# Attention and a gated two-layer block in one kernel: TensorE in written order, another order of loads, transposes and constants

## The chip, the cores and the metric

The kernel runs on one core of one Trainium2 chip. A core has five engines that run their own instruction streams and wait for each other by semaphores: TensorE (PE in the profile, its weight loads PEld), VectorE (DVE), ScalarE (ACT), GpSimd (POOL) and SyncE (SP), which here only issues DMAs. TensorE writes to PSUM, of which there are eight banks. The metric is the time of one execution on the device, in microseconds (us).

## What is computed

The input is q, k and v of 4 batches, 8 heads, 768 positions and 64 dimensions. Each head attends causally; heads 0, 2 and 6 ("retrieval") see all earlier positions, the other five ("streaming") only the first 4 positions and a window of 64. The result, 3072 rows of 512, goes through two dense layers with a swish between them.

```python
def _attn_ref(q, k, v, is_retrieval, n_sink, window):
    scores = scale * np.matmul(q, k.transpose(0, 1, 3, 2))
    ...
    stream_keep = causal & (is_sink | in_win)
    mask = np.where(retr[0, :, 0, 0, None, None], full_mask, stream_mask)
    scores = np.where(mask[None, :, :, :], scores, -1000000000.0)
    ...
    a = a / (np.sum(a, axis=-1, keepdims=True) + 1e-09)
    return np.matmul(a, v).astype(np.float32)

def _moe_ref(x, w_in, w_out, beta):
    h = x @ w_in                                   # 3072 x 512 by 512 x 2048
    g = h * (1.0 / (1.0 + np.exp(-beta * h)))
    return (g @ w_out).astype(np.float32)          # 2048 x 512
```

## The kernel before

The work is cut into eight units, one for each batch and half of the sequence (384 positions): unit 0 is batch 0, first half; unit 1 its second half, and so on. Even units have less attention than odd ones, since a first half sees fewer keys. For a unit there are these pieces:

- Loads. `load_qk` brings q and k of a pair of heads as two DMAs of 192 KB and casts each to bf16 (tiles `q2`, `k2`). `load_v` brings v by head and casts it on GpSimd into `vr` (retrieval) and `vs` (streaming, where the four first positions, `sk`, are copied into every block).
- `transpose_pair` turns q and k of a pair on TensorE by the identity `ident`, six matmuls into one PSUM tile, and copies it on VectorE to `QK`. For streaming heads VectorE then gathers the key blocks into `KX` in two copies, the second for the sinks. There are four pairs a unit.
- `scores_round` makes scores into a PSUM tile `sp`, ScalarE takes the exponential into `es`, VectorE multiplies it by a mask. `BURSTS` groups these rounds: three groups in an even unit, five in an odd one.
- `sums` adds up the exponentials on TensorE (the matrix `esel` puts each head's sum in a row of `misc`), VectorE takes the reciprocal `rec`, and five DMAs bring it to all partitions: three small ones from `rec` to `rd` in DRAM, then two of 384 KB from `rd` to `R`. SyncE issues them.
- `pv` multiplies the exponentials by v into two `sp` tiles; VectorE multiplies by `R` into `xT`, the unit's activations, in two instructions.
- `mm1` has 16 steps. A step is four matmuls into an `h` tile, ScalarE's tanh into `t`, and one instruction of VectorE, (t+1)*h, into `gT`. (The swish is written as a tanh, with beta halved, and the output is halved at the end.) An `h` buffer is free once `gT` has been made.
- `mm2` has 48 matmuls into an `o` tile, 16 for each of three blocks of 128 rows; then ScalarE copies `o` to `osb`, and SyncE issues the DMA of 256 KB to the output.

PSUM is split into two `sp` tiles of two banks, one `misc`, two `h` and one `o`. Both weight matrices are loaded once, in four slices of 1 MB each through the tile `wf`, and cast: `w_in` on VectorE, `w_out` on GpSimd.

After unit 0's attention, a loop runs nine times over 16 steps. In turn n, each step issues one step of unit n's `mm1`, three matmuls of unit n-1's `mm2`, and the pieces that `pieces_a(n + 1)` (transposes at steps 0 to 2, rounds from step 1, sums at 9, `pv` at 13 and 14) and `pieces_l(n + 2)` (loads) put at that step. This is the order in which the program is written. What each engine gets is decided by the scheduler of the layer below, which reorders the instructions by its own estimates of cost, on all engines, TensorE included, and puts in every wait. SyncE's queue also carries all loads but the first unit's k and four of its v loads, which ScalarE issues. Each DMA takes one of eight semaphores in turn, and waits until the DMA that had that semaphore before it has landed, whichever engine issued that one.

The program begins with unit 0's loads; the constants (`ident`, the masks, `esel`, `beta_h`) come after them.

Of the kernel before, what the change touches and what calls it, by code (L numbers as in the profile page):

```python
# [20 lines left out]
NQ = 384  # L21
# [31 lines left out]
def kernel(  # L53
# [29 lines left out]
    inp = pool("inp", 2)  # L83
# [25 lines left out]
    def load_qk(b, u, pi):  # L109
        ha, hb = PAIRS[pi]  # L110
        res = []
        for nm, src in (("q2", q), ("k2", k)):
            f = stg.tile([128, 2, TU, D], F32, name=nm + "f", bufs=4)
            eng = nc.scalar if (b, u, nm) == (0, 0, "k2") else nc.sync
            eng.dma_start(
                out=f,
                in_=bass.AP(src.tensor, src.offset + ((b * H + ha) * S + u * NQ) * D,
                            [[TU * D, 128], [(hb - ha) * S * D, 2], [1, TU * D]]),
            )
            c = inp.tile([128, TU, 2, D], BF16, name=nm)  # L120
            cast(nc.gpsimd if b > 0 and nm == "q2" else nc.vector, c.rearrange("p t a d -> p a t d"), f)
            res.append(c)
        qk_in[b, u, pi] = res
# [30 lines left out]

    for pi in range(NP):
        load_qk(0, 0, pi)
    for f in load_v(0, 0):
        f()
# [42 lines left out]

    beta_h = consts.tile([128, FO], F32, name="beta_h")
    nc.scalar.dma_start(out=beta_h, in_=moe_beta.rearrange("(fo fi) -> fi fo", fi=128))
    nc.vector.tensor_scalar(out=beta_h, in0=beta_h, scalar1=0.5, scalar2=None, op0=MULT)

# [5 lines left out]
    def load_w_in(s):  # L211
        f = stg.tile([128, 4, FS], F32, name="wf")
# [7 lines left out]
        cast(nc.vector, w_in_sb[:, :, s * FS:(s + 1) * FS], f)  # L220

    def load_w_out(s):
        f = stg.tile([128, 4, FS], F32, name="wf")
        nc.sync.dma_start(out=f, in_=moe_w_out[s * 512:(s + 1) * 512, :].rearrange("(fo fi) d -> fi fo d", fi=128))
        cast(nc.gpsimd, w_out_sb[:, s * 4:(s + 1) * 4, :], f)
# [4 lines left out]
    def transpose_pair(x, pi):  # L230
        b, u = x.b, x.u
        c2 = qk_in.pop((b, u, pi))
        if (b, u) == (0, 0):
            ps = ps_h.tile([128, 2, TU, 128], BF16, name="h")
        else:
            ps = ps_m.tile([128, 2, TU, 128], BF16, name="misc")
        for i, c in enumerate(c2):
            for t in range(TU):
                nc.tensor.transpose(ps[:, i, t, :], c[:, t, :, :].rearrange("p a d -> p (a d)"), ident)  # L239
        nc.vector.tensor_copy(  # L240
            out=QK[pi][:, :, u * NQ:(u + 1) * NQ].rearrange("d a (p t) -> d a p t", t=TU),
            in_=ps.rearrange("d a t p -> d a p t"))
# [84 lines left out]
    def sums(x):  # L327
# [23 lines left out]
        for j in range(TU):  # L351
            nc.sync.dma_start(out=rd[:, j, :], in_=rec[32 * j:32 * j + 8, :])
        R = rp.tile([128, NP, NQ], F32, name="R")
        src = rd[:]
        for i in range(2):
            nc.sync.dma_start(
# [29 lines left out]
    def mm1(x, fi):  # L386
        if fi == 0:
            x.gT = gp.tile([128, FO, NQ], BF16, name="gT")
        h = ps_h.tile([128, 512], F32, name="h")
# [7 lines left out]
    def mm2(x, step, last):  # L397
        for m in range(step * 3, step * 3 + 3):
            ns, fi = divmod(m, FO)
            if fi == 0:  # L400
                x.o = ps_s.tile([128, 2, 512], F32, name="sp")[:, 0, :] if last else ps_o.tile([128, 512], F32, name="o")
            nc.tensor.matmul(x.o, x.gT[:, fi, ns * 128:(ns + 1) * 128], w_out_sb[:, fi, :],  # L402
                             start=(fi == 0), stop=(fi == FO - 1))
            if fi == FO - 1:
                osb = op_.tile([128, d_model], F32, name="osb")
                nc.scalar.activation(out=osb, in_=x.o, func=AF.Copy, scale=0.5)  # L406
                r0 = x.b * S + x.u * NQ + ns * 128
                nc.sync.dma_start(out=out[r0:r0 + 128, :], in_=osb)
# [5 lines left out]
    def pieces_a(n):  # L414
# [3 lines left out]
        x = units[n]  # L418

        def t(pi):  # L420
            return lambda: transpose_pair(x, pi)

        def burst(bu):
            def f():
                for (pi, ri) in bu:
                    scores_round(x, pi, ri)
            return f
        bs = BURSTS[x.u]
        p = [(0, t(0)), (0, t(1)), (1, t(2)), (1, burst(bs[0])), (2, t(3))]
        rest = bs[1:]  # L430
        for i, bu in enumerate(rest):
            p.append((3 + (6 * i) // len(rest), burst(bu)))
        p.append((9, lambda: sums(x)))
        p += [(13, lambda: pv(x, 0)), (14, lambda: pv(x, 2))]
        return p

    def pieces_l(n):

        if n >= N:
            return []  # L440
        x = units[n]
        p = [(2 * pi, lambda pi=pi: load_qk(x.b, x.u, pi)) for pi in range(NP)]
        p += [(5 + i, f) for i, f in enumerate(load_v(x.b, x.u))]
        return p

    for s, f in pieces_a(0):
        f()
    for s in range(4):
        load_w_in(s)
    for s, f in pieces_l(1):  # L450
        f()
    for s in range(4):
        load_w_out(s)
    for n in range(N + 1):
        lists = [pieces_a(n + 1), pieces_l(n + 2)]
        for s in range(FO):
            for l in lists:
                for st, f in l:
                    if st == s:
                        f()  # L460
            if n < N:
                mm1(units[n], s)
            if n > 0:
                mm2(units[n - 1], s, n == N)
# [35 lines left out]
```

The softmax here doesn't subtract the row's maximum and nothing guards it: scores larger than these inputs give would overflow.

## Time and profile before

| | |
|---|---|
| median of 2 runs | 297.25 us (295.93 to 298.58) |
| the profiled execution | 295.16 us, of which 293.4 us are the span from its first to its last instruction |
| busy: PE, DVE, ACT, POOL | 244.4, 176.2, 131.5, 74.1 us |
| moved by DMA | 44.97 MB, 153 GB/s over the span |
| first transpose on TensorE | 10.50 us |
| first `rec` | 29.27 us |
| first `mm1` matmul | 42.28 us |
| `xT` of units 1, 2, 3 | 83.23, 107.54, 134.35 us |
| `mm2` of the last unit alone | 279.63 to 289.36 us |

Matmuls are pipelined, so the length that a row gives to one of them (331 ns for `mm1`) is not what it takes from the next; four `mm1` matmuls that follow each other take 0.65 us from start to start, three of `mm2` take 0.65. Rows give an engine's idle time before them and what ended it; such idle time costs something only where the engine is what the others wait for.

### The profile page before, as it was taken

The numbers are of one execution on the slowest core, as the hardware profiler recorded it, in microseconds if no ns is written. First come the engines' busy times: TensorE is split into PE (matmuls) and PEld (weight loads), VectorE is DVE, ScalarE is ACT, GpSimd is POOL, SyncE is SP. The second block draws the span as 40 slices with busy tenths as digits, with TensorE's granted clock in tenths as the row PEclk, the third lists the DMA queues.
The fourth block names the chain that finished last, engine by engine and source line by source line (L and its number), as shares of the span: only waits on it lengthen the run. The fifth ranks groups of instructions, "written<-read, shape, count | busy, mean of one in ns | idle before, by whom it ended". The sixth has DMA issues, their size and how long they took to land.

```text
span 293.4 us, 5696 instructions
## 1 busy us (share of the span) xinstructions
PE 244.4 (83%) x2196; PEld 128.0 (44%) x2196; DVE 176.2 (60%) x335; ACT 131.5 (45%) x217; POOL 74.1 (25%) x158
## 2 busy tenths in 40 slices
PE   0137129799799989998999979999999999999994
PEld 0124104454345534554455534554455455545541
DVE  1186429985848896627963696449754975353400
ACT  0123006743147529624644487336643684245421
POOL 1291001756342254103460261053000000000000
PEclk9999857999999999999999999999999999999999
DMA  7993699989796799087786879434014110500111
GB/s 217 179 236 101 157 243 275 266 298 330 170 234 183 173 270 264 4 185 198 179 222 153 197 187 224 95 87 143 36 42 106 38 38 8 140 36 36 38 71 71
DMA packets 75850, 44.97 MB, mean 153 GB/s; under 512 B 47984, under 2 KB 68656, under 8 KB 75824
## 3 DMA queue, kind: packets, MB, share of 16 engines
q1 hardware_dynamic: 69536, 43.04, 58.6%
q10 hardware_dynamic: 6288, 1.58, 3.0%
q8 instruction: 17, 0.28, 0.4%
q14 instruction: 9, 0.07, 0.1%
HBM read 38.22 MB, written 6.39 MB: 152 GB/s over the span
## 4 chain that ended last, share of the span: by engine, by line
PE 55%; DVE 18%; DMA 12%; ACT 5%; issue 3%; POOL 3%; SPq 1%; ACTq 0%; DVEq 0%; POOLq 0%
PE h L391 23%; PE o L402 17%; PE sp L382 5%; DMA k2f<-in_k_dram 4%; PE sp L402 4%; DVE gT L395 4%; PE misc L343 3%; DMA wf<-in_moe_w_in_dram 3%; PE sp L309 3%; ACT t L394 3%; DMA R<-rd 2%; DVE QK_214 L240 2%; DMA vf<-in_v_dram 2%; DVE xT L383 2%; POOL vs L103 1%
## 5 line engine op out<-in xcount | busy, mean ns | idle before, releaser
L391 PE MATMUL h<-xT,w_in_sb 128*128 128x384 bf16 x512 | 107.1, 331 | 17.3 <-DVE xT L383 13.4
L394 ACT ACTIVATE t<-h,beta_h 128x384 f32<-128x384 f32 x128 | 74.6, 586 | 104.1 <-PE h L391 102.3
L395 DVE SCALAR_TENSOR_TENSOR gT<-t,h 128x384 bf16<-128x384 f32 x128 | 69.9, 550 | 61.0 <-ACT t L394 60.4
L402 PE MATMUL o<-w_out_sb,gT 128*128 128x512 bf16 x336 | 92.3, 379 | 3.5 <-ACT osb L406 3.4
L391 PEld LDWEIGHTS <-w_in_sb 128*128 128x128 bf16 x512 | 46.1, 98 | 58.2 <-issue 25.4
L402 PEld LDWEIGHTS <-gT 128*128 128x128 bf16 x384 | 36.5, 98 | 37.4 <-issue 6.4
L103 POOL CAST vs<-vf 128x384 bf16<-128x384 f32 (+1 forms) x40 | 22.6, 574 | 47.1 <-DMA vf<-in_v_dram 33.1
L103 POOL CAST vr<-vf 128x192 bf16<-128x192 f32 x24 | 9.1, 386 | 52.2 <-DMA vf<-in_v_dram 51.7
L383 DVE TENSOR_TENSOR xT<-sp,R 128x768 bf16<-128x768 f32 x16 | 14.6, 950 | 10.8 <-DMA R<-rd 9.6
L406 ACT ACTIVATE osb<-o 128x512 f32<-128x512 f32 x21 | 12.5, 594 | 15.2 <-PE o L402 12.7
L103 POOL CAST vs<-sk 4x640 bf16<-4x640 f32 (+3 forms) x24 | 17.3, 745 | 0.0
L343 PEld LDWEIGHTS <-esel 128*32 128x32 bf16 x372 | 9.0, 97 | 7.4 <-issue 7.0
L402 PE MATMUL sp<-w_out_sb,gT 128*128 128x512 bf16 x48 | 10.8, 379 | 0.0
L382 PEld LDWEIGHTS <-vr 128*64 128x64 bf16 x108 | 7.8, 112 | 6.5 <-issue 5.0
L349 DVE RECIPROCAL rec<-misc 96x128 f32<-96x128 f32 x8 | 7.6, 954 | 4.8 <-PE misc L343 4.8
L382 PEld LDWEIGHTS <-vs 128*64 128x64 bf16 x260 | 8.6, 116 | 3.0 <-issue 3.0
L239 PE MATMUL h<-ident,q_104 128*128 128x128 bf16 x3 | 0.5, 298 | 10.5 <-DVE ident L164 10.5
L103 POOL CAST w_out_sb<-wf 128x2048 bf16<-128x2048 f32 x4 | 7.6, 1892 | 5.4 <-DMA wf<-in_moe_w_out_dram 5.4
L309 PE MATMUL sp<-QK_218 64*128 64x384 bf16 (+2 forms) x36 | 8.4, 302 | 0.3 <-ACT es_1_668 L311 0.3
L309 PE MATMUL sp<-QK_212 64*128 64x384 bf16 (+2 forms) x72 | 8.4, 304 | 0.3 <-ACT es_1_556 L311 0.3
L103 DVE CAST w_in_sb<-wf 128x2048 bf16<-128x2048 f32 x4 | 4.8, 1210 | 4.9 <-DMA wf<-in_moe_w_in_dram 4.1
L240 DVE COPY QK_212<-misc 128x768 bf16<-128x768 bf16 x7 | 6.6, 946 | 0.4 <-PE misc L239 0.4
(484 smaller groups left out, 266.7 us busy)
## 6 DMA issues: line engine op xcount, KB each, us to landing
q2f<-in_q_dram SPq DMA_DIRECT2D x32, 192.0 KB
R<-rd SPq DMA_DIRECT2D x16, 384.0 KB
out_dram<-osb SPq DMA_DIRECT2D x24, 256.0 KB
k2f<-in_k_dram SPq DMA_DIRECT2D x28, 192.0 KB
vf<-in_v_dram SPq DMA_DIRECT2D x20, 224.0 KB
wf<-in_moe_w_out_dram SPq DMA_DIRECT2D x4, 1024.0 KB
vf<-in_v_dram SPq DMA_DIRECT2D x16, 192.0 KB
vf<-in_v_dram SPq DMA_DIRECT2D x24, 96.0 KB
```

Of the source, the lines that this page charges most:

```text
L103: eng.tensor_copy(out=dst, in_=src)
L240: nc.vector.tensor_copy(out=QK[pi][:, :, u * NQ:(u + 1) * NQ].rearrange("d a (p t) -> d a p t", t=TU), in_=ps.rearrange("d a t p -> d a p t"))
L309: nc.tensor.matmul(o[j][0], o[j][1], o[j][2], start=True, stop=True)
L343: nc.tensor.matmul(sm[32 * j:32 * j + 32, 0:128], esel[:, hpos, :, :].rearrange("p a b -> p (a b)"), e, start=(done[j] == 0), stop=(done[j ...
L349: nc.vector.reciprocal(rec, sm[0:96, 0:128])
L382: nc.tensor.matmul(a, l, r, start=st, stop=sp)
L383: nc.vector.tensor_mul(x.xT[:, p0:p0 + 2, :], o[:, :, 0:NQ], x.R[:, p0:p0 + 2, :])
L391: nc.tensor.matmul(h[:, 0:NQ], w_in_sb[:, pi, fi * 128:(fi + 1) * 128], x.xT[:, pi, :], start=(pi == 0), stop=(pi == NP - 1))
L394: nc.scalar.activation(out=t, in_=h[:, 0:NQ], func=AF.Tanh, scale=beta_h[:, fi:fi + 1])
L395: nc.vector.scalar_tensor_tensor(out=x.gT[:, fi, :], in0=t, scalar=1.0, in1=h[:, 0:NQ], op0=ADD, op1=MULT)
L402: nc.tensor.matmul(x.o, x.gT[:, fi, ns * 128:(ns + 1) * 128], w_out_sb[:, fi, :], start=(fi == 0), stop=(fi == FO - 1))
L406: nc.scalar.activation(out=osb, in_=x.o, func=AF.Copy, scale=0.5)
```

## The change

TensorE's instructions are issued in the order of the program (`manual_schedule` with that engine); the other engines are scheduled as before. The loop is written anew. A `slot` runs 16 steps of one unit's `mm1`, of another's `mm2`, or of both; the first two slots have `mm1` alone, then there is one with unit 0's `mm2` alone, and from unit 2 on both go together. Transposes stand a slot ahead of the scores that use them, `rec` at step 10, both halves of `pv` at step 14. Where a slot has `mm1` alone, every third `h` is taken from the `o` bank; where it has `mm2` alone, `o` is taken from the `h` banks. Constants stand ahead of all loads; q and k of unit 1 ahead of `w_in`. `rd` and `R` are issued by ScalarE. Some casts change engines.

```diff
-    inp = pool("inp", 2)
+    inp = pool("inp", 4)
...
-            cast(nc.gpsimd if b > 0 and nm == "q2" else nc.vector, c.rearrange("p t a d -> p a t d"), f)
+            cast(nc.gpsimd if (b, u) == (0, 1) or b > 0 and nm == "q2" else nc.vector, c.rearrange("p t a d -> p a t d"), f)
...
-    for pi in range(NP):
-        load_qk(0, 0, pi)
-    for f in load_v(0, 0):
-        f()
...
+    for pi in range(NP):
+        load_qk(0, 0, pi)
     beta_h = consts.tile([128, FO], F32, name="beta_h")
...
+    for f in load_v(0, 0):
+        f()
...
-        f = stg.tile([128, 4, FS], F32, name="wf")
+        f = stg.tile([128, 4, FS], F32, name="wf", bufs=3)
...
-        cast(nc.vector, w_in_sb[:, :, s * FS:(s + 1) * FS], f)
+        cast(nc.vector if s % 2 else nc.gpsimd, w_in_sb[:, :, s * FS:(s + 1) * FS], f)
...
-        if (b, u) == (0, 0):
+        if b == 0:
             ps = ps_h.tile([128, 2, TU, 128], BF16, name="h")
...
-        nc.vector.tensor_copy(
+        cast(
+            nc.scalar if (b, u) == (0, 0) and pi % 2 else nc.vector,
...
-            nc.sync.dma_start(out=rd[:, j, :], in_=rec[32 * j:32 * j + 8, :])
-        R = rp.tile([128, NP, NQ], F32, name="R")
+            nc.scalar.dma_start(out=rd[:, j, :], in_=rec[32 * j:32 * j + 8, :])
+        R = rp.tile([128, NP, NQ], F32, name="R", bufs=1)
...
-            nc.sync.dma_start(
+            nc.scalar.dma_start(
                 out=R[i * D:(i + 1) * D],
...
+        if alone and fi % 3 == 2:
+            h = ps_o.tile([128, 512], F32, name="o")
+        else:
+            h = ps_h.tile([128, 512], F32, name="h")
...
+            x.o = ps_h.tile([128, 512], F32, name="h") if alone else ps_o.tile([128, 512], F32, name="o")
...
+    def slot(m1, m2, extras, pre=0):
+        done = 0
+        for s in range(FO):
+            if s == 0 and m2 is not None:
+                while done < pre:
+                    mm2(units[m2], done, m1 is None)
+                    done += 1
+            for st, f in extras:
+                if st == s:
+                    f()
+            if m1 is not None:
+                mm1(units[m1], s, m2 is None)
+            if m2 is not None:
+                while done < pre + ((3 * FO - pre) * (s + 1)) // FO:
+                    mm2(units[m2], done, m1 is None)
+                    done += 1
...
+    with tc.manual_schedule(engines={mybir.EngineType.PE}):
+        for f in (tr(0, 0), tr(0, 1), burst(0, 0), tr(0, 2), burst(0, 1), tr(0, 3), burst(0, 2)):
+            f()
+        for pi in range(NP):
+            load_qk(0, 1, pi)
+        for s in range(4):
+            load_w_in(s)
+        for f in (sm(0), tr(1, 0), tr(1, 1), burst(1, 0), tr(1, 2), burst(1, 1), tr(1, 3), burst(1, 2), pvs(0)):
+            f()
+        for f in load_v(0, 1):
+            f()
+        for pi in range(NP):
+            load_qk(1, 0, pi)
+        for s in range(4):
+            load_w_out(s)
+        slot(0, None, [(0, burst(1, 3)), (2, burst(1, 4)), (5, sm(1)), (14, pvs(1))] + loads(2, 99, 0))
+        slot(1, None, [(9 + i, tr(2, i)) for i in range(NP)] + loads(3, 0, 5))
+        slot(None, 0, [(0, burst(2, 0)), (4, burst(2, 1)), (8, burst(2, 2)), (12, sm(2))]
+             + [(12 + i, tr(3, i)) for i in range(NP)])
+        for n in range(2, N):
+            a = n + 1
+            ex = loads(n + 2, 0, 5)
+            if n == 2:
+                ex.append((0, pvs(2)))
+            if a < N:
+                nb = len(BURSTS[units[a].u])
+                at = [1, 4, 7] if nb == 3 else [0, 2, 4, 6, 8]
+                ex += [(at[i], burst(a, i)) for i in range(nb)] + [(10, sm(a)), (14, pvs(a))]
+            if a + 1 < N:
+                ex += [(11 + i, tr(a + 1, i)) for i in range(NP)]
+            slot(n, n - 1, ex, pre=9 if n == 2 else 3)
+        slot(None, N - 1, [])
```

Here `tr`, `burst`, `sm`, `pvs` and `qk` stand for `transpose_pair`, the rounds of one group, `sums`, both halves of `pv`, and `load_qk` of a unit; `loads(n, q0, v0)` puts unit n's `load_qk` at steps q0, q0+1, ... and its v loads at v0, v0+1, ...

## The prediction

> **What bounds the kernel now.** I read the slices of the page first, and cut the span into stages by them.
>
> ```profile
> PE   0137129799799989998999979999999999999994
> PEclk9999857999999999999999999999999999999999
> DMA  7993699989796799087786879434014110500111
> ```
>
> One digit is 7.3 us. TensorE is the bound from about 42 us on. Ahead of that it waits for loads, with the DMA engines mostly at 7 to 9 tenths. Next, busy time by stage, cut about where VectorE makes a unit's xT (its attention output); columns are the stage, its length, busy time of each engine, TensorE's clock, DMA share, GB/s:
>
> ```profile
> 42.28:83.23 40.95, 35.81 (x324) 18.30 (x324) 31.69 (x58) 17.26 (x28) 18.52 (x24) 0.93 1.01 267
> ...
> 134.35:164.79 30.44, 28.62 (x248) 14.90 (x248) 20.79 (x43) 15.21 (x26) 11.99 (x23) 1.00 0.74 183
> 164.79:196.00 31.21, 29.00 (x293) 15.54 (x292) 20.25 (x39) 16.57 (x27) 9.02 (x18) 1.00 0.70 169
> 196.00:227.00 31.00, 30.01 (x261) 15.65 (x259) 21.83 (x44) 16.10 (x27) 5.69 (x10) 1.00 0.27 77
> 227.00:257.40 30.40, 29.46 (x295) 15.79 (x294) 19.87 (x38) 17.28 (x29) 0.51 (x1) 1.00 0.20 54
> ```
>
> The four steady stages hold units 4 to 7's attention and take 123.05 us; TensorE is busy 117.1 of them, so written order has at most 6 us to win there. What follows 257.40 is MoE alone, 36.0 us. Third, the rows of VectorE and of SyncE's queue that one steady stage shows, and those of the last unit (start, length, row):
>
> ```profile
> 171.34 0.94 DVE L240 COPY QK_216<-misc 128x768 bf16<-128x768 bf16 x1
> ...
> 172.66 0.61 DVE L249 COPY KX_1_2389<-QK_216 128x896 bf16<-128x896 bf16 x1
> ...
> 184.77 0.95 DVE L349 RECIPROCAL rec<-misc 96x128 f32<-96x128 f32 x1 [0.88 <-PE misc L343]
> ...
> 185.75 0.98 SPq L352 DMA_DIRECT2D rd<-rec  x3
> ```
>
> ```profile
> 248.97 1.25 SPq L356 DMA_DIRECT2D R<-rd  x2
> ...
> 255.65 1.82 DVE L383 TENSOR_TENSOR xT<-sp,R 128x768 bf16<-128x768 f32 x2 [1.60 <-DMA R<-rd]
> ```
>
> The reciprocal's way back: sums end at 245.25, R lands at 255.65, 10.4 us later, with DMA at 0.20; with xT 12.2. Last, the waits:
>
> ```profile
> PE o L402 <- ACT osb L406: 3.4, 6, 0.7
> ```
>
> Of 24 changes of the output accumulator TensorE feels six, 0.57 us each: the scheduled order puts other matmuls in between.
>
> **Steady slots, step by step.** Slot n is 16 steps, each with a step of unit n's mm1 (0.65 us: chain pieces "PE h L391 x4"), three matmuls of the mm2 of the unit before (0.65: "PE o L402 x3") and a share of the next unit's attention. #11 is step 11 of a slot. TensorE now runs exactly what is written; the other engines are still scheduled, and their new order is what costs.
>
> First, VectorE. In slots 3, 4 and 5 its order after step 10 is: four pieces of transposes 0 and 1, then the QK copy of transpose 2, a k cast, the KX copies, and only then the gT of #11, #12 and #13. Transpose 2 stands on TensorE before mm1 #13, which needs the h buffer that gT #11 frees. So TensorE stands still for 0.87 (QK copy) + 0.27 (k cast) + 0.53 (KX) + 0.16 (its sinks) + 0.5 (gT), each from its start to the next row's, with 0.1 for the signals = 2.4 us; in slot 5, without casts, 2.0. Nothing covers it: mm2 #13 stands behind mm1 #13.
>
> Second, ScalarE. The five DMAs of rd and R move there from SyncE. Behind t #10 come three rd issues (0.98), which wait for the reciprocal (0.95 after the sums), then osb, then R (1.25), which waits for rd. osb frees the only `o` buffer, and matmul 32 of mm2 follows matmul 31 at once. TensorE reaches it 0.97 after the sums (mm1 0.76 after other operands, one matmul 0.21); osb ends at 0.1+0.95+0.98+0.6 = 2.65. A stall of 1.7, in slots 3 to 6. Queued behind R are t #11 to #13; in slots 3 to 5 their gT is late anyway, in 6 the two h buffers just cover them. SyncE, which waited 37.4 us for reciprocals, issues its loads sooner: worth nothing here, since no steady wait of TensorE names a load.
>
> The Trainium skill, "DMA: Bandwidth & Descriptors", section "Issuing engines are not separate DMA queues", says that issuing from several engines saves only sequencer time, usually small beside the transfer. The row disagrees on small: 0.98+1.25 us per unit is more than three t activations. By the rule as written this edit costs nothing, and the time below would be 298.
>
> Third, the other two accumulator changes: at matmul 16 osb stands behind two exps (0.75 each) and t #4, about 1.1 us; at the slot's end, with the last matmul just done, 0.16 for its end, 0.6 for osb, 0.04: 0.8. The stalls are 2.4+1.7+1.1+0.8 = 6.0 in slots 3 and 4, 5.6 in 5, 3.6 in 6: 21.2 us. Busy time stays 117.1, less 1.1 for three transposes of unit 4 done a slot earlier (6 matmuls take 0.38). Slots 3 to 6 take 137.2, 14 more than now. Bounds: from 121.9 (stalls as now) to 142.
>
> **The head.** Constants first: the diagonal mask's select runs at 14.80 on GpSimd, behind casts that wait 7.82 us for v; mask_c follows at 15.12, the first QK copy at 16.34. Now the copy can start at 11.0, because TensorE's first transpose at 10.50 does not move: the identity cast stands behind beta's scaling, whose DMA wait (4.50 us) is kept. The streaming masks, made until 22.9, drop out too. The reciprocal moves from 29.27 to about 21, R's issue to about 25.5. It then lands 6.6 (last unit) to 8.7 us (32.5 to 41.2) later, and unit 0's xT is ready at 34 to 36. But its mm1 also waits, from the fourth step, on VectorE for the cast of the fourth w_in slice, now behind q and k of unit 1: by bytes, 9.4 MB with R at 267 GB/s, 37 us. Now mm1 starts at 42.28, so 5 us are won; between that and none if the loads run at 222 GB/s (the mean of 10 to 20 us). The edits beside this (unit 1's casts on GpSimd, 8 of 0.46; two QK copies on ScalarE; three weight buffers) lie in the time of these loads.
>
> Slot 0 and slot 1 run mm1 alone, with a third buffer. One buffer's turn is 0.86 (mm1 start to t) + 0.61 + 0.55 + 0.05 = 2.07, a third of it 0.69 a step, 11 us. Slot 0 ends with unit 1's R: sums about 6.5 in, plus 12.2: 37+18.7 = 56. Slot 1 adds transposes and copies: 11+4, 71. By bytes it is 76: VectorE's order in slot 1 holds k casts of unit 3, behind 19.8 MB (q, k 1.57 MB a unit, v 1.28 or 1.44, weights 8.4, R 1.6) at 267 GB/s, plus 1.85 for the first packet. I take 74; the ends are 71 and 91 (at 222 GB/s). The mm2-alone slot reaches its sums after 12 steps of mm2 (7.8) and unit 2's scores and sums (2.2+0.9); then R's way of 12.2 rules, longer than the 8.9 of matmuls left: 74+7.8+3.1+12.2 = 97. Slot 2: mm1 10.4, 39 mm2 8.4, unit 3's scores, sums and products 2.9+1.4+2.5, transposes 1.5, changes of operand 0.6, three matmuls ahead of slot 3 0.65, accumulator waits 1.9: 30.3, so unit 3's mm1 starts at 127.5. Now it starts at 135.36, with 2.2 us less done: the head gains 10.
>
> The loads' order has no other place on the path; R with one buffer waits for a product that ends a slot earlier; w_in casts on GpSimd (1.9 each for 1.23) lie beside loads, and cost 1.9 if they are late. If the load waits of rd and R (each waits for an earlier load on its semaphore) come late, ScalarE stands still; in the steady slots those loads are due over 10 us before.
>
> **The sum.** 127.5 + 137.2 + 36.0 = 300.7 us of span. The profiled execution took 295.16, 1.76 over its span of 293.4, and the median of the runs, 297.25, is 2.1 over that: 300.7+1.8+2.1 = 304.6, say 305.
>
> The clock: it fell to 0.70 and 0.62 in 30 to 50 us, around 11.8 us without matmuls. The Trainium skill, "TensorE: Matmul & The Clock Gate", section "What's actually happening", halves it after an idle window of about 3.4 us. By that rule the new gaps of 2.4 us cost no clock; no row here shows a gap of that size by itself.
>
> **Rivals.** *Stalls covered* (faster): TensorE in written order has no more waits than now, because gT #11 comes before transpose 2's copies matter. Slots 3 to 6 take 121.9: 127.5+121.9+36.0+3.9 = 289. For it: transposes are a slot ahead and cost no QK wait at the slot's start. Against: the order on VectorE. The point: mm1 #13 within 0.5 us of transpose 2. *Half* (no change): the slots' stalls are half as long, 129.5 for 137.2: 297. *ScalarE held by loads* (slower): in slots 0 and 1 rd and R wait for loads of the next units, and VectorE for k casts, so that the mm2-alone slot starts halfway from 76 to 91: 9.5 later, 314. For it, the 19.8 MB; against, 330 GB/s in one slice.
>
> **How the numbers follow.** 305 as worked out: 0.48, by itself 300 to 310. Stalls covered: 0.18. Half: 0.17. Held by loads: 0.17. Two per cent, 291.3 to 303.2, is about what a measurement of this kernel tells from no change. A quarter of the first case falls under 303.2, so same has 0.17+0.12 = 0.29, slower 0.53, faster 0.18. The range leaves out about a tenth at each end, half of *covered* and half of *held*: 290 to 316.
>
> **What would show it.** Right: TensorE waits for gT for over 2 us between transpose 2 and mm1 #13 in slots 3 to 5; TensorE waits for osb longer than 1.5 us behind rd; steady slots of 34 us; unit 3's mm1 at 122 to 133 us. Wrong: steady slots under 31 us, or unit 3's mm1 before 118.

## The result, and the profile after

The changed kernel takes 326.59 us (median of two runs, 326.57 to 326.61) against 297.25: a ratio of 1.099, with a 95% interval of 1.078 to 1.120. It is slower, as the prediction's likeliest case had it, but by 29 us instead of 8. All medians and ratios below leave out executions in which the chip was disturbed, while the two marks of dve_written come from one such; ratios are to the kernel before, run on the same chip beside each kernel.

The profiled execution took 326.57 us with a span of 324.6. Its slices:

```profile
PE   0347329569788669996895898769876989799895
PEclk9999999987999959999899799999999999999999
DMA  7999797699985995979525730140005000410011
```

A slice is now 8.1 us. TensorE has more to do early than before (its first transpose comes no earlier, at 11.28 us after 10.50), but it has holes up to the middle of the span, and still eights and sixes where there were nines. Busy time by stage, cut at unit 0's, 1's, 2's and 3's `xT` and then at the starts of units 3 to 7's `mm1` (columns as above):

```profile
0.00:45.00 45.00, 15.91 (x185) 10.62 (x186) 23.40 (x42) 11.58 (x15) 20.09 (x63) 1.00 0.98 220
45.00:71.20 26.20, 19.67 (x204) 11.35 (x204) 14.99 (x26) 11.76 (x20) 8.36 (x16) 0.93 0.81 202
71.20:114.70 43.50, 32.70 (x280) 17.51 (x280) 30.02 (x56) 15.07 (x25) 23.61 (x35) 0.96 0.92 231
114.70:148.90 34.20, 31.04 (x295) 16.26 (x295) 17.95 (x35) 17.97 (x29) 11.36 (x24) 0.90 0.87 202
151.80:185.60 33.80, 28.10 (x240) 14.97 (x240) 19.72 (x39) 13.78 (x23) 4.37 (x11) 0.90 0.55 132
185.60:220.50 34.90, 28.79 (x299) 15.80 (x298) 20.68 (x40) 17.39 (x28) 5.29 (x12) 1.00 0.26 70
220.50:254.50 34.00, 27.91 (x256) 15.28 (x254) 21.77 (x39) 15.43 (x26) 4.53 (x8) 1.00 0.17 48
254.50:288.60 34.10, 29.78 (x287) 15.54 (x286) 15.69 (x30) 19.14 (x31) 0.00 (x0) 1.00 0.17 48
```

Slots 3 to 6 take 136.8 us, 13.8 more than before, with TensorE as busy as it was (114.6 against 117.1 us): what was added is waiting. (From xT to xT, as in the table below, it is 136.9 against 121.3.) The other half of the loss is the head. Unit 3's `xT` comes at 148.93 instead of 134.35. The rest, MoE alone, is 36.0 us again.

What TensorE waits for in the whole span, and the rows of one steady slot that answer to those shown of before:

```profile
PE o L405 <- ACT osb L409: 17.8, 17, 1.8
PE h L395 <- DVE gT L399: 15.9, 8, 2.8
```

```profile
170.99 0.97 ACTq L353 DMA_DIRECT2D rd<-rec  x3
172.00 0.60 ACT L409 ACTIVATE osb<-o 128x512 f32<-128x512 f32 x1 [0.67 <-DVE gT L399]
172.65 0.38 PE L405 MATMUL o<-w_out_sb,gT 128*128 128x512 bf16 x1 [1.72 <-ACT osb L409]
173.07 1.91 ACTq L357 DMA_DIRECT2D R<-rd  x2
...
178.10 0.61 DVE L250 COPY KX_1_2285<-QK_153 128x896 bf16<-128x896 bf16 x1
...
178.83 1.01 DVE L399 SCALAR_TENSOR_TENSOR gT<-t,h 128x384 bf16<-128x384 f32 x2
179.43 0.97 PE L395 MATMUL h<-xT,w_in_sb 128*128 128x384 bf16 x4 [2.80 <-DVE gT L399]
```

`osb` stands behind `rd`, and TensorE waits 1.72 us; then `gT` stands behind transpose 2's copies, and TensorE waits 2.80. Last, the way of `R` in the head, from the chain of waits (start, length, what):

```profile
27.75 5.33 DMA rd<-rec
...
33.89 10.97 DMA R<-rd
...
58.86 12.29 DMA R<-rd
...
107.39 7.25 DMA R<-rd
...
141.49 7.41 DMA R<-rd
```

### The profile page after: what moved, and what is told of

Same layout as the page of the kernel before. It is cut to its first block, busy times and chain, and to the rows that moved or that the text cites. A ratio compares the mean times of both kernels' runs of the same rounds, so it can differ in the third digit from the quotient of the medians.

```text
span 324.6 us, 5708 instructions
## 1 busy us (share of the span) xinstructions
PE 245.0 (75%) x2196; PEld 132.5 (41%) x2196; DVE 175.9 (54%) x323; ACT 134.8 (42%) x219; POOL 80.1 (25%) x168
## 4 chain that ended last, share of the span: by engine, by line
PE 53%; DMA 20%; DVE 13%; ACT 7%; issue 4%; ACTq 2%; POOL 0%; SPq 0%; DVEq 0%
PE h L395 20%; PE o L405 17%; DMA R<-rd 12%; PE h L405 5%; PE sp L310 4%; ACT osb L409 3%; PE sp L383 2%; DMA beta_h<-in_moe_beta_dram 2%; DVE xT L384 2%; DMA k2f<-in_k_dram 2%; PE misc L344 2%; DVE gT L399 2%; ACT t L398 2%; DMA rd<-rec 2%; DMA q2f<-in_q_dram 2%
## 5 line engine op out<-in xcount | busy, mean ns | idle before, releaser
L395 PE MATMUL h<-xT,w_in_sb 128*128 128x384 bf16 x472 | 100.0, 339 | 18.9 <-DVE gT L399 15.9
L398 ACT ACTIVATE t<-h,beta_h 128x384 f32<-128x384 f32 x118 | 68.3, 581 | 105.4 <-PE h L395 99.4
L405 PE MATMUL o<-w_out_sb,gT 128*128 128x512 bf16 x288 | 82.8, 388 | 17.8 <-ACT osb L409 17.8
L399 DVE SCALAR_TENSOR_TENSOR gT<-t,h 128x384 bf16<-128x384 f32 x118 | 64.6, 552 | 57.7 <-ACT t L398 56.6
L395 PEld LDWEIGHTS <-w_in_sb 128*128 128x128 bf16 x512 | 48.2, 100 | 70.2 <-issue 39.6
L405 PE MATMUL h<-w_out_sb,gT 128*128 128x512 bf16 x96 | 22.1, 379 | 0.0
L310 PE MATMUL sp<-QK_149 64*128 64x384 bf16 (+2 forms) x72 | 9.7, 355 | 4.9 <-DVE xT L384 3.9
L409 ACT ACTIVATE osb<-h 128x512 f32<-128x512 f32 x6 | 3.6, 598 | 17.8 <-PE h L405 17.8
L103 POOL CAST w_out_sb<-wf 128x2048 bf16<-128x2048 f32 x4 | 7.6, 1893 | 13.6 <-DMA wf<-in_moe_w_out_dram 13.6
L239 PE MATMUL h<-ident,q_159 128*128 128x128 bf16 x3 | 0.5, 296 | 11.3 <-DVE ident L159 11.3
L395 PE MATMUL o<-xT,w_in_sb 128*128 128x384 bf16 x40 | 8.8, 346 | 0.2
L398 ACT ACTIVATE t<-o,beta_h 128x384 f32<-128x384 f32 x10 | 5.8, 581 | 7.5 <-PE o L395 7.2
(490 smaller groups left out, 294.8 us busy)
```

Of the source, the lines that this page charges most:

```text
L103: eng.tensor_copy(out=dst, in_=src)
L310: nc.tensor.matmul(o[j][0], o[j][1], o[j][2], start=True, stop=True)
L395: nc.tensor.matmul(h[:, 0:NQ], w_in_sb[:, pi, fi * 128:(fi + 1) * 128], x.xT[:, pi, :], start=(pi == 0), stop=(pi == NP - 1))
L398: nc.scalar.activation(out=t, in_=h[:, 0:NQ], func=AF.Tanh, scale=beta_h[:, fi:fi + 1])
L399: nc.vector.scalar_tensor_tensor(out=x.gT[:, fi, :], in0=t, scalar=1.0, in1=h[:, 0:NQ], op0=ADD, op1=MULT)
```

## Experiments

Two marks stand for each kernel: unit 3's `xT` (the end of the head) and the time from there to unit 7's `xT` (slots 3 to 6), both from the profiled execution. Four kernels with one and the same program ahead of slot 2 (after, dve_written, o_changes, dve_o) had unit 2's `xT` at 114.7, 115.7, 111.3 and 110.3 us, so the first mark is good to some 5 us, and small differences are read from the medians.

| Kernel | unit 3's xT | slots 3 to 6 | median | ratio to before |
|---|---|---|---|---|
| before | 134.4 | 121.3 | 297.3 | |
| after | 148.9 | 136.9 | 326.6 | 1.099 (1.078 to 1.120) |
| no_written_order | 145.4 | 118.6 | 302.4 | 1.013 (1.006 to 1.019) |
| r_on_sync | 152.1 | 123.7 | 317.0 | 1.062 (1.055 to 1.069) |
| no_order_sync | 139.1 | 116.6 | 295.0 | 0.988 (0.981 to 0.995) |
| before_r_act | 146.5 | 122.6 | 308.7 | 1.033 (1.024 to 1.042) |
| before_rd_act | 133.2 | 123.2 | 295.5 | 0.990 (0.983 to 0.997) |
| before_consts | 134.4 | 121.1 | 294.8 | 0.987 (0.980 to 0.993) |
| dve_written | 148.7 | 134.6 | 319.6 | 1.070 (1.059 to 1.082) |
| o_changes | 144.1 | 130.3 | 313.6 | 1.051 (1.044 to 1.058) |
| dve_o | 143.5 | 134.8 | 317.5 | two executions |
| o_sync | 154.2 | 127.1 | 316.3 | 1.065 (1.059 to 1.072) |
| early_sync | 147.8 | 115.7 | 303.1 | 1.015 (1.009 to 1.021) |
| no_w_out | 140.3 | 137.2 | 319.6 | 1.088 (1.081 to 1.094) |
| q1_on_dve | 143.7 | 137.2 | 322.0 | one execution |
| free_merged | 141.8 | 120.4 | 300.7 | 1.006 (1.002 to 1.010) |
| free_merged_sync | 135.3 | 118.0 | 289.8 | 0.968 (0.960 to 0.977) |
| free_merged_sync_lord | 127.9 | 117.7 | 286.3 | 0.958 (0.950 to 0.965) |
| all_written | 136.9 | 116.7 | 293.2 | two executions |
| head_free | 130.6 | 115.3 | 285.8 | 0.957 (0.950 to 0.964) |

**Which edits cost: TensorE's order and R's queue.** These runs undo one edit, or do one alone, or undo two together.

no_written_order gives TensorE's order back to the scheduler:

```diff
-    with tc.manual_schedule(engines={mybir.EngineType.PE}):
+    with ExitStack():
```

> The changed kernel with TensorE's order left to the scheduler, all else kept. Theory D (the head is lost to loaded bytes that R's packets stand behind, and to R's way with nothing beside it): unit 3's xT stays at 143 to 150 us (148.9 now); slots 3 to 6 fall to 125 to 131 since the scheduler fills the waits, time 310 to 319. Rival W (the written order of TensorE costs the head): unit 3's xT at 138 or earlier, time under 306.

302.4 us: 24 of the 29 us come back with this one edit. Its slots 3 to 6 by stage, xT to xT:

```profile
145.40:176.60 31.20, 28.72 (x245) 15.04 (x246) 23.34 (x43) 14.47 (x25) 12.37 (x23) 0.90 0.77 187
176.60:206.00 29.40, 28.50 (x296) 15.41 (x295) 18.70 (x38) 16.78 (x28) 3.87 (x9) 1.00 0.47 115
206.00:235.70 29.70, 28.57 (x255) 15.13 (x254) 21.11 (x42) 15.08 (x26) 3.65 (x6) 1.00 0.20 55
235.70:264.00 28.30, 27.97 (x275) 14.32 (x274) 13.81 (x27) 17.07 (x28) 0.00 (x0) 1.00 0.21 57
```

TensorE is busy 113.8 of 118.6 us, with `rd` and `R` still on ScalarE: in a free order their issues cost the slots some 2 us at most (116.6 with SyncE's queue, below). The head keeps most of its loss (145.4), as theory D had it. The slots and the time do not fit D: 118.6 instead of 125 to 131, and a time that only rival W allowed.

r_on_sync puts the five DMAs back:

```diff
-            nc.scalar.dma_start(out=rd[:, j, :], in_=rec[32 * j:32 * j + 8, :])
+            nc.sync.dma_start(out=rd[:, j, :], in_=rec[32 * j:32 * j + 8, :])
...
-            nc.scalar.dma_start(
+            nc.sync.dma_start(
                 out=R[i * D:(i + 1) * D],
```

> The five DMAs of rd and R go back to SyncE, all else as in the changed kernel. Theory H (the head is lost because rd and R run on ScalarE's queue beside SyncE's loads, and R and loads wait for each other on shared semaphores): unit 0's R lands at 38 to 41 us instead of 44.9, unit 1's way from reciprocal to xT falls from 15.9 to 12 or 13, unit 3's mm1 starts at 138 to 145 instead of 151.8, time 308 to 318. Rival W (the head is lost to TensorE's written order or to the order of loads): unit 3's mm1 stays within 148 to 155, and only the osb wait behind rd in slots 3 to 6 shrinks from 1.7 to about 1 us each, time 321 to 327.

Neither theory: the time is H's, the head is W's. Slots 3 to 6 fall by 13.2 us: TensorE's waits for `gT` in them go from 10.3 to 2.6 us, so stall A, which the prediction put down to VectorE's order alone, went with the queue. The head does not move. The chain of waits shows that R's own DMA did become short:

```profile
40.56 6.04 DMA R<-rd
...
73.00 5.91 DMA R<-rd
...
114.31 6.08 DMA R<-rd
...
145.42 6.55 DMA R<-rd
```

But unit 0's `R` was issued at 39.93 only, because `rd`, on SyncE behind w_in's loads, took 7.31 us to land. From the reciprocal to xT it took 21.2 us in unit 0 and 20.3 in unit 1, longer than on ScalarE's queue (19.1 and 15.9), and TensorE in written order stood 15.0 and 10.2 us for these two xT. no_order_sync does both edits.

> TensorE's order left to the scheduler, rd and R on SyncE. Theory W2 (the queue of rd and R costs only because TensorE's written order feels the waits it makes): 299 to 305, slots 3 to 6 at 117 to 121 as in the run without written order (118.6). Rival H (ScalarE's queue costs by itself): time under 297.

295.0 us, on rival H's side, and slots of 116.6. Queue and order together: 326.6 with both edits, 317.0 without the queue, 302.4 without the order, 295.0 without either. Written order costs 22 to 24 us with either queue, and ScalarE's queue 7 to 10 with either order. The queue alone on the kernel before:

> The kernel before with rd and R on ScalarE, nothing else. Theory W2: within 2% of before, 295 to 302, steady slots of 30 to 31.5 us. Rival H: slots over 32, time 304 or more.

308.7 us: the time is rival H's, the slots are theory W2's, as before (122.6). The loss is in the head, where the chain of waits has

```profile
33.91 9.96 DMA R<-rd
...
69.68 8.12 DMA R<-rd
...
100.92 9.90 DMA R<-rd
...
136.86 9.52 DMA R<-rd
```

against 5.9 to 6.6 us on SyncE in the fence above. In the steady stage, with no load beside it, `R` takes 6.18 us on ScalarE's queue too (at 202.12). What TensorE waits for xT from 40 us to unit 3's mm1, in the kernel before and then in this one:

```profile
PE h L391 <- DVE xT L383: 13.4, 4, 11.8
PE h L391 <- DVE xT L383: 18.4, 2, 14.3
```

Ahead of the mm1 of units 0 to 3 it stands 14.29, 4.09, 3.54 and 3.03 us here (the last two end with a `gT` that VectorE makes right behind xT), against 11.79, 0.23, 0.36 and 1.05 before: 11.5 us more, of the 12.1 by which unit 3's xT is later. And SyncE's loads wait for `R` and `rd` in turn, on semaphores that they share; its queue's waits in this kernel:

```profile
SPq L115 <- DMA R<-rd: 11.4, 3, 5.2
SPq L115 <- DMA rd<-rec: 5.0, 1, 5.0
```

In the kernel before, loads wait 3.0 us for `R` and none for `rd`. before_rd_act moves `rd` alone:

> The kernel before with the three small rd DMAs on ScalarE, R's two on SyncE. Theory Q (the queue costs because R's 0.8 MB on ScalarE's own ring share the DMA engines with the loads of SyncE's: R took 8 to 10 us there, 6 to 6.6 on SyncE): R's time back at 6 to 8.7 us, unit 3's xT at 133 to 138, time 296 to 301. Rival V (ScalarE or a load's semaphore is what is waited for at the first of the five DMAs): unit 3's xT at 141 or later, time 304 or more.

295.5 us, where theory Q had it: five DMAs cost 10 us, the three small ones of them nothing. Rival V, that the first of the five is where the wait lies, is out. SyncE's queue waits for `rd` before it issues `R` (13.6 us in four waits), and no load is issued in these waits. What was not told apart is which half of it costs more once `R` is on ScalarE: R's bytes beside the loads, or the loads that wait for R's landing.

before_consts moves only the constants ahead of the loads:

> The kernel before with the constants ahead of the loads, nothing else. By the prediction's step the first QK copy starts at 11 to 12 us instead of 16.3 and unit 0's reciprocal at 21 to 24 instead of 29.3; if its xT follows, 291 to 295. Rival: R of unit 0 then stands behind more loaded bytes and lands no earlier than 40 us, time 296 to 299.

294.8 us, a gain of 1.3%. The reciprocal came at 26.1 instead of 29.3, not at 21 to 24, and xT at 39.3 instead of 41.3. So constants win some 3 us, order and queue lose 32 together, and the rest of the change makes no difference in sum (295.0 with it, 294.8 without).

**Why written order costs in the steady slots.** dve_written keeps VectorE in written order too, from slot 2 on:

```diff
-            slot(n, n - 1, ex, pre=9 if n == 2 else 3)
+            with tc.manual_schedule(engines={mybir.EngineType.PE, mybir.EngineType.DVE}):
+                slot(n, n - 1, ex, pre=9 if n == 2 else 3)
```

> VectorE too is kept in written order from slot 2 on, so that gT #11 and #12 come before the copies of transpose 2; TensorE's order is unchanged. Theory S (stall A is this order): the wait of 2.8 us for gT between transpose 2 and mm1 #13 goes in slots 3 to 5, slots of 31.5 to 32.5 instead of 33.8 to 34.9, time 318 to 321. Rival (the stall comes back as another wait, of xT, KX or t): slots still over 33.3, time 324 to 327.

319.6 us, as theory S said, but the slots, at 33.6 us each, are the rival's, and part of the wait came back: t #11 now waited behind R's issue on ScalarE. Stall A had two covers, and only one was taken off. o_changes moves the accumulator changes:

```diff
+    UPTO = [3, 6, 9, 12, 16, 19, 22, 25, 28, 32, 35, 38, 41, 44, 46, 48]
...
-            if s == 0 and m2 is not None:
+            if s == 0 and m2 is not None and not (m1 is not None and pre == 3):
...
-                while done < pre + ((3 * FO - pre) * (s + 1)) // FO:
+                while done < (UPTO[s] if m1 is not None and pre == 3 else pre + ((3 * FO - pre) * (s + 1)) // FO):
```

> In slots 3 to 6 the last matmul of each output accumulator stands at the end of a step, with a step of mm1 and the next round before the next accumulator's first matmul, none of mm2 stands ahead of a slot's first mm1, and the second osb stands ahead of rd on ScalarE. VectorE's order, which is scheduled, changes with it: gT #11 moves ahead of the copies of transpose 2. Theory S (stalls B, C and D are 3.6 us a slot, and A goes with VectorE's order): slots 3 to 6 take 120 to 126 instead of 136.8, time 310 to 316. Rival (TensorE is simply slower in written order, the waits move elsewhere): slots 3 to 6 over 132, time over 321.

and dve_o joins the two edits:

> Both edits: the accumulator changes of the run above and VectorE in written order from slot 2 on. Theory S: all four stalls gone, slots 3 to 6 take 119 to 124, waits of TensorE for osb under 3 us in the whole run instead of 17.8, time 308 to 314; the head unchanged, unit 3's mm1 at 150 to 152. Rival: slots 3 to 6 over 130, time over 320.

The waits for osb went (17.8 to 1.1 us), but the slots gave back 6.6 us instead of 11 to 17 in the one, and 2.1 in the other, where theory S had all four stalls gone. Neither theory S held on the slots; in dve_o the rival's "over 130" did. VectorE's rows at the ends of three of dve_o's steady slots show what is late instead, with the `gT` behind the last and TensorE's row after it:

```profile
176.94 1.82 DVE L384 TENSOR_TENSOR xT<-sp,R 128x768 bf16<-128x768 f32 x2 [3.67 <-DMA R<-rd]
...
244.11 1.82 DVE L384 TENSOR_TENSOR xT<-sp,R 128x768 bf16<-128x768 f32 x2 [2.78 <-DMA R<-rd]
...
278.28 1.82 DVE L384 TENSOR_TENSOR xT<-sp,R 128x768 bf16<-128x768 f32 x2 [3.89 <-DMA R<-rd]
280.02 1.01 DVE L399 SCALAR_TENSOR_TENSOR gT<-t,h 128x384 bf16<-128x384 f32 x2
```

```profile
280.62 0.81 PE L395 MATMUL h<-xT,w_in_sb 128*128 128x384 bf16 x4 [2.65 <-DVE gT L399]
```

TensorE reaches the slot's end sooner, `R` lands no sooner, and VectorE stands idle for it with the next `gT` queued behind. o_sync has o_changes' accumulators and takes `rd` and `R` off ScalarE:

> The accumulator changes at the ends of steps (as in o_changes) and rd and R on SyncE (as in r_on_sync). Theory S2 (slots 3 to 6 lose by three things only: osb waits, t waiting behind R's issue on ScalarE, and gT behind the copies of transposes on VectorE; the first two hold a slot back singly, so each has to go): slots 3 to 6 take 116 to 121 us, xT to xT, against 136.9 in the changed kernel and 123.7 with rd and R on SyncE alone; unit 3's xT stays at 150 to 153; time 308 to 312. Rival (TensorE in written order has other waits that come up next): slots 3 to 6 at 123 or more, time 314 or more.

Missed again: 127.1 and 316.3 us, the rival, and no better than r_on_sync, which keeps the old accumulator changes (123.7 and 317.0). In all four slots xT started 6.9 to 7.5 us after R's issue, which is R's landing, and 9.8 to 11.6 after the reciprocal. From sums at step 10, TensorE has five and a half steps and the products to put beside that. So early_sync keeps the edits of o_sync and moves the scores and sums up:

```diff
-    UPTO = [3, 6, 9, 12, 16, 19, 22, 25, 28, 32, 35, 38, 41, 44, 46, 48]
+    UPTO = [3, 6, 9, 12, 16, 20, 24, 28, 32, 34, 36, 38, 41, 44, 46, 48]
...
-                at = [1, 4, 7] if nb == 3 else [0, 2, 4, 6, 8]
+                at = [0, 2, 5] if nb == 3 else [0, 1, 3, 4, 6]
...
-[(10, sm(a)), (14, pvs(a))]
+[(8, sm(a)), (14, pvs(a))]
```

> As the run with the accumulator changes and SyncE's queue (o_sync, 316.3 us, slots 3 to 6 in 127.1), TensorE in written order, but the next unit's scores pulled forward and its sums at step 8 instead of 10. Theory F (with the three waits gone, R's way sets the slot's length: from the sums at step 10 only 5.5 steps and the products lie beside some 11 us, so xT is late, and gT and the next scores behind it): slots 3 to 6 take 116 to 120.5, time 304 to 309. Rival (written order loses in many small places, whatever the sums): 124 or more, time 313 or more.

```profile
147.80:177.70 29.90, 29.06 (x280) 16.20 (x275) 21.93 (x40) 15.01 (x26) 10.46 (x21) 1.00 0.75 181
177.70:206.80 29.10, 27.30 (x276) 14.71 (x276) 19.85 (x40) 17.52 (x29) 4.87 (x10) 1.00 0.39 101
206.80:235.20 28.40, 27.61 (x276) 15.39 (x270) 20.86 (x39) 14.65 (x25) 5.60 (x9) 1.00 0.21 57
235.20:263.50 28.30, 27.98 (x282) 15.12 (x282) 15.75 (x31) 17.55 (x29) 0.00 (x0) 1.00 0.21 58
```

Theory F, and a little better than its ranges: 115.7 us in written order, as good as the scheduler's 116.6, and 13 us off the time. In these slots TensorE's waits for xT and `gT` fell from 10.9 us (o_sync) to 2.6. The floor was R's way. The four stalls of the prediction were real, but they lay on top of it: taking them off let TensorE run into it.

**What holds the head.** no_w_out leaves out loads:

```diff
-        nc.sync.dma_start(out=f, in_=moe_w_out[s * 512:(s + 1) * 512, :].rearrange("(fo fi) d -> fi fo d", fi=128))
-        cast(nc.gpsimd, w_out_sb[:, s * 4:(s + 1) * 4, :], f)
+        cast(nc.gpsimd, w_out_sb[:, s * 4:(s + 1) * 4, :], w_in_sb[:, :, s * FS:(s + 1) * FS])
```

> The four loads of w_out (4.2 MB) are left out; w_out's tile is filled by GpSimd from w_in's, so the output is not the reference's. Theory D: R of unit 1 lands 6 to 9 us after its issue instead of 12.3, its xT at 64 to 68 instead of 71.2, and units 2 and 3 follow, unit 3's xT at 139 to 145 instead of 148.9, time 317 to 321. Rival (R's way is as long without these bytes, or the head is held by other things): unit 1's xT at 70 or later, unit 3's at 147 or later, time over 323.

Theory D: unit 1's `xT` comes at 64.6, 8.5 us after R's issue, where the four kernels named above took 11.3 to 13.4. Unit 3's comes at 140.3, where those four spread from 143.5 to 148.9, so in the head as a whole the gain is hardly more than that spread. The slots keep their 137.2. q1_on_dve gives unit 1's casts back to VectorE (the condition `(b, u) == (0, 1)` goes):

> Unit 1's eight casts go back from GpSimd to VectorE. Theory P (a multiply of VectorE that took 3.36 us instead of 0.56 stood beside six casts of GpSimd): that multiply takes 0.5 to 0.9 us and unit 0's reciprocal starts at 22 to 24.5 us instead of 25.8, unless the casts themselves wait for their loads on VectorE; time 323 to 327, since unit 0's xT is set by R behind loads. Rival (the long multiply has another cause): over 2 us again.

The multiply took 0.55 us (theory P), but the reciprocal was no earlier (26.4): the casts waited for their loads on VectorE, as the expectation had left open.

free_merged joins the two slots that have `mm1` or `mm2` alone, with TensorE's order free:

```diff
-        slot(1, None, [(9 + i, tr(2, i)) for i in range(NP)] + loads(3, 0, 5))
-        slot(None, 0, [(0, burst(2, 0)), (4, burst(2, 1)), (8, burst(2, 2)), (12, sm(2))]
-             + [(12 + i, tr(3, i)) for i in range(NP)])
+        slot(1, 0, [(0, tr(2, 0)), (0, tr(2, 1)), (1, tr(2, 2)), (2, tr(2, 3))] + loads(3, 0, 5)
+             + [(2, burst(2, 0)), (4, burst(2, 1)), (7, burst(2, 2)), (10, sm(2)), (14, pvs(2))]
+             + [(11 + i, tr(3, i)) for i in range(NP)], pre=3)
```

> TensorE's order left to the scheduler, and mm1 of unit 1, mm2 of unit 0 and unit 2's attention together in one slot, as before the change, instead of in two slots one after the other. Theory M (what is left of the head's loss is this split: with mm1 or mm2 alone in a slot, R's way of unit 2 has too little beside it): unit 2's xT at 100 to 105 us instead of 112.4, unit 3's at 132 to 138 instead of 145.4, time 290 to 296. Rival L (the loads hold the head, whatever the slots): unit 3's xT at 143 or later, time 299 or more.

300.7 against 302.4, nearer to rival L; with `R` on ScalarE the split hardly matters. With SyncE it does:

> TensorE's order free, rd and R on SyncE, and one slot for mm1 of unit 1, mm2 of unit 0 and unit 2's attention. Theory: the steady slots keep 116 to 118, the head gains 2 to 5 us over the run with the split slots (unit 3's xT at 134 to 137 instead of 139.1): 290 to 293. Rival (the split costs nothing): 294 to 297.

289.8 against 295.0. With the old order of loads on top (`load_w_in` ahead of `load_qk(0, 1, pi)`, `load_w_out` ahead of `load_qk(1, 0, pi)`):

> The same with the order of loads as before the change: w_in ahead of unit 1's q and k, w_out ahead of unit 2's. Theory (the order of loads sets unit 0's xT, 39.3 us in the kernel before with constants first and 44.6 with the new order): unit 0's xT at 39 to 42, 2 to 4 us less than the run beside it, 287 to 291. Rival (what unit 0 gains, unit 1 loses): within 1.5 us of the run beside it.

286.3, and unit 3's `xT` at 127.9, but the two intervals overlap, so these 3.5 us are likely, not shown. Unit 0's xT (44.1) is earlier than in the run beside it (47.4), but no earlier than no_order_sync had it with the new order (44.6): the theory's reason is not shown, though its time was right. This kernel is 4.2% faster than before.

**Can written order do it?** all_written is early_sync with the joined slot (its sums at step 9) and the old order of loads; head_free is the same with TensorE's order written from slot 2 on only (and sums at step 10 in the joined slot).

> TensorE in written order throughout, with every cause found so far taken out: rd and R on SyncE, one slot for mm1 of unit 1 with mm2 of unit 0, the old order of loads, accumulator changes at the ends of steps, sums at step 8 (9 in that first full slot). If written order costs only through where its pieces stand, slots 3 to 6 take 115 to 118 and the time is 282 to 292, level with the scheduler's 286.3. Rival (written order loses in the head, where loads come when they come): unit 3's xT at 136 or later instead of 127.9, time 293 or more.

> The same, but TensorE's order is written only from slot 2 on; the head is left to the scheduler. Unit 3's xT at 126 to 131, slots 3 to 6 in 115 to 118: 281 to 287. Rival (the scheduler's order of the steady slots, 117.7, is as good or better): 287 to 290.

293.2 and 285.8. In the slots written order is level (116.7 and 115.3); in the head it loses. At the start of slot 1, all_written's TensorE and then head_free's:

```profile
77.17 1.66 PE L395 MATMUL h<-xT,w_in_sb 128*128 128x384 bf16 x4 [9.57 <-DVE xT L384]
```

```profile
73.52 3.61 PE L405 MATMUL o<-w_out_sb,gT 128*128 128x512 bf16 x16 [0.69 <-ACT osb L409]
77.66 0.48 PE L395 MATMUL h<-xT,w_in_sb 128*128 128x384 bf16 x2 [0.52 <-DVE xT L384]
```

xT comes at about the same time in both, 76.2 and 76.6, but in the 14 us ahead of it the scheduler had put nearly all of unit 0's mm2 and unit 2's four transposes. The written order has two of these transposes there and the rest behind mm1 #0, so TensorE stands still for 9.57 us.

## Why the prediction was half right

**Steady slots: right.** 137.2 us for slots 3 to 6 against 136.8. Stall A: 2.4 predicted (2.0 in slot 5), 2.80, 2.53 and 2.46 in slots 3 to 5. Stall B: 1.7, measured 1.71 to 1.77 in all four. C and D: 7.6 together; the waits for osb in these slots are 14.4 us, less 7.0 of B, 7.4. What follows took the 36.0 us that were said. The signs named (slots of 34 us, TensorE for gT over 2 us, for osb over 1.5) all came. But the stalls were not each worth their own price: the four kernels that took them away with the sums left at step 10 won 2 to 10 us in these slots, because R's way from sums at step 10, which the prediction had worked out as 12.2 us and not laid against the rest of the slot, was a floor just under them.

**The head: wrong, and the whole miss.** Unit 3's mm1 was to start at 127.5 and started at 151.8, past the bound at 133. Term by term: mm1 of unit 0 at 47.4 instead of 37 (10.4); slots 0 and 1 44.0 instead of 37 (7.0); the slot of mm2 alone 25.7 instead of 23 (2.7); slot 2 34.7 instead of 30.5 (4.2).

The step that failed is R's way in the head: "It then lands 6.6 (last unit) to 8.7 us later" for unit 0, and "plus 12.2" for the units after. From the reciprocal to the start of xT the 12.2 is 10.4 (the rest is xT itself). In the head it was 19.1 us in unit 0 and 15.9 in unit 1 (12.9 and 12.4 in units 2 and 3). The 10.4 came from the last unit, with DMA at 0.20, and the kernel before had a row against it that the prediction passed over: unit 1's reciprocal at 61.71 and its xT at 83.23, 21.5 us. Beside loads the way is long on either queue, for different reasons. On ScalarE's queue `R` itself is long, 10.97, 12.29, 7.25 and 7.41 us. On SyncE's, `R` takes some 6 us, but `rd` and `R` stand behind loads, and the two ways took 21.2 and 20.3 us (r_on_sync). So ScalarE's queue is not by itself what made the head late in written order: with `R` back on SyncE, unit 3's xT was no earlier.

The sentence on SyncE's queue, that its loads go sooner and that this is "worth nothing here", looked at the steady slots alone. In the head ScalarE's queue does cost where TensorE's order is free: `R` then shares the DMA engines with loads, and loads wait for `R` too. before_r_act shows this without any other edit (of the 252 GB/s moved during unit 0's `R`, R's own 768 KB in 9.96 us make some 79), and before_rd_act that it hangs on `R` and not on `rd`.

What this cost is less than its length. Unit 0's mm1 started 21.5 us after the reciprocal instead of 16, which makes 5.5 of its 10.4; the late reciprocal makes the other 4.8. For the xT of units 1 and 2 TensorE stood 2.6 and 3.6 us. In slot 2 its clock was then at 0.77, 0.50, 0.50 and 0.52 in the windows of 2 us from 114 to 122: up to 3.4 us more, where the prediction had put the clock at nothing. The rest of the 24.3 us was not told apart.

Two smaller terms of the head were off as well. The reciprocal of unit 0 came at 25.8, not 21: constants first gave 3.2 us in before_consts, and in the changed kernel VectorE's multiply beside GpSimd's casts took 2.8 longer than alone (where it took 1.60, in dve_o, the reciprocal came at 24.16). And the slots with mm1 or mm2 alone, which the prediction summed as they stood, leave R's way bare; joined, with SyncE's queue, they gave 5.2 us.

**The rivals.** *ScalarE held by loads* came nearest in time (314) and named the place, slots 0 and 1, but not all of the mechanism. ScalarE did stand 4.06 us in unit 0 until `rd` had landed, and TensorE 3.99 behind it, but TensorE then stood 7.68 more for xT; `R` ran beside the loads, and SyncE's loads waited for `R` (10.2 us). VectorE did wait for a k cast's load, 1.86 us at 60.2, with TensorE 2.32 behind it. *Stalls covered* and *half* are out. The rule weighed on issuing engines, the Trainium skill's "DMA: Bandwidth & Descriptors", section "Issuing engines are not separate DMA queues", has two halves: the sequencer time saved is small, and DMAs of different issuers interleave on the same engines. The prediction disputed the first. In a free order the page is right: before_rd_act moved three of the five issues and lost nothing. In written order the prediction was: the issues were stall B, and with them on SyncE the same wait for osb fell from 1.7 to 1.16 us. The second half bears on the 7 to 10 us that the queue cost. Its section "Queues, rings and completion order" says that each DMA engine takes its queues in turn, packet by packet, which agrees with R's 7.3 to 12.3 us beside loads in the head and 6.18 without; no run here shows the turns themselves.

What stays open: which wait of the head costs how much beyond this. Order and queue act on each other there (unit 3's xT at 148.9 with both edits, 152.1 with the order alone, 145.4 with the queue alone and 139.1 with neither), and single executions differ by 5 us.

## What to carry to other kernels

Before a small DMA on the critical path is moved to another engine's queue, look at what its old queue was holding back: a queue that waits also keeps its later loads out of the way, and on shared semaphores they may wait for the moved one. Take a latency from rows of the stage in which it will stand: from the reciprocal to xT it was 10.4 us in the last unit and 16 to 21 beside loads. When an engine's order is written by hand, lay every latency of the slot (here sums to xT, 12 us) against the work that stands beside it, first of all those that no row shows as a wait because the scheduler had filled them. And price waits by the floor under them: a stall that is taken away is worth only the distance to the next thing that is late.

## What the hardware showed

**The clock falls after some gaps of 2.5 to 2.8 us.** Around the 2.80 us gap in slot 3 (176.63 to 179.43), windows of 2 us of the changed kernel (TensorE's clock is the third figure from the end):

```profile
178.00:180.00 2.00, 0.57 (x4) 0.37 (x4) 1.81 (x5) 0.00 (x0) 0.00 (x0) 0.98 1.11 200
180.00:182.00 2.00, 2.00 (x9) 0.57 (x9) 0.56 (x1) 0.58 (x1) 0.00 (x0) 0.50 1.09 287
182.00:184.00 2.00, 2.00 (x46) 1.82 (x43) 1.16 (x2) 0.00 (x0) 0.23 (x1) 0.66 0.49 143
184.00:186.00 2.00, 2.00 (x14) 1.12 (x12) 2.00 (x3) 0.58 (x1) 2.00 (x5) 1.00 0.28 65
```

The clock was halved for about 3.4 us right after it (0.66 is half speed for two thirds of a window), and again for as long after a gap of 2.49 us at 149.3, but not after those of 2.53 and 2.46 us at 213.2 and 247.1. The prediction took the Trainium skill's "TensorE: Matmul & The Clock Gate", section "What's actually happening", to say that gaps of 2.4 us cost no clock; two of these four did. The section says too that its window runs freely. That would fit these rows, where nearly the same gap costs or not, but no run here moves a gap to test it.

**A VectorE multiply takes six times as long beside GpSimd's casts.** In the changed kernel, VectorE's multiply and the first of six casts that GpSimd did meanwhile, back to back until 22.6 us; then the same multiply in q1_on_dve:

```profile
18.88 3.36 DVE L318 TENSOR_TENSOR es_0_286<-es_0_286,mask_s_124 128x768 bf16<-128x768 bf16 x1 [0.28 <-ACT es_0_286 L312]
19.53 0.50 POOL L103 CAST q_332<-q2f 128x384 bf16<-128x384 f32 x1
```

```profile
22.39 0.55 DVE L318 TENSOR_TENSOR es<-es,mask_s 128x768 bf16<-128x768 bf16 x1
```

3.36 us against 0.55. Beside the same casts it took 3.27 us in r_on_sync and in o_changes, and 2.82 in o_sync. The casts had been moved to GpSimd, and were called free in the prediction because they lay beside loads.
